# Four more columns summed on TensorE, stores issued by ScalarE, softmax steps set between product and sums

## The chip, the cores and the metric

One core of a Trainium2 chip runs the whole program. The metric is the device time of one execution in microseconds (us). Before the change the median of 6 runs is 426.52 us (425.56 to 428.74).

The engines named here: TensorE (PE, multiplies matrices; PEld is its loading of weights), VectorE (DVE), ScalarE (ACT), GpSimd (POOL) and SyncE (SP). The last three also issue DMA transfers, each on a queue of its own.

## The reference

`x` is 8 x 4160 x 192 and `weight_gen` 8 x 4160 x 8 x 7. The first part is a causal convolution whose weights differ at each position and for each of 8 heads of 24 channels; the second a maxout layer.

```
w   = softmax(weight_gen over its 7 taps)
y[b, s, h, :] = sum over k of w[b, s, h, k] * x[b, s - 6 + k, h, :]      # zeros ahead of s = 0
g   = maximum(y @ w1, y @ w2)              # w1, w2: 192 x 1024, 33280 rows
out = g @ w_out                            # w_out: 1024 x 192
```

## The kernel before, in words

**Layout.** The 33280 positions are split over 128 partitions, so each partition holds 260 consecutive positions, called columns. Columns are worked on in batches of 16 (17 batches, the last of 4). `pieces(b)` cuts a batch into parts, and `UNITS` lists them: batch 0 in four units of 4 columns, batch 1 in 4, 4 and 8, the others in 8 and 8, the last one of 4. A unit is what one product, one set of sums and one transposition handle.

**Softmax.** For a batch, `exp_sum` takes the exponentials on ScalarE (L126), `red` sums them over the taps on VectorE (L131), `ln` takes the logarithm on ScalarE (L134), `shift` subtracts it on VectorE (L139), and `weights` takes the exponential again on ScalarE (L147), now the finished weight in bf16, each value twice.

**Convolution.** `mul` multiplies seven shifted views of `x` by the weights into `m_t` (VectorE, L158). `adds` sums the seven taps in three instructions: taps 0 to 2 with 3 to 5 (L174), then L179, then L181, which writes `y_t`. The tile `m_t` has room for one batch and is taken anew from its pool (`pm`, one buffer) for every batch; L158 of a new batch therefore depends on the readers of the tile before it.

**Transposition.** TensorE needs the channels on the partitions. Most units are transposed by a DMA that SP issues (`transpose`, L190, from `y_t` to `yt`). The first six units, columns 0 to 23, take another way, `sum_transpose`: TensorE multiplies `m_t` by an identity matrix and sums the taps in PSUM as it goes (L220), and ScalarE copies the result (L225). For units 0 to 3 it sums all seven taps, for units 4 and 5 four, after VectorE's first sum only.

**Maxout.** max(y w1, y w2) w_out is computed as y (w1 w_out) + relu(y (w2 - w1)) w_out. A "tile" is an eighth of the hidden layer for a unit of 8 columns (for a unit of 4, two eighths for half of the columns); there are 260 tiles. `hid_tile` computes one on TensorE into PSUM (L252), `relu` brings it to SBUF on ScalarE (L262). When all tiles of a unit are there, `out_first` and `out_second` compute its columns of the result on TensorE (L304 with y, L292 with the relu), and `evac` copies them from PSUM to `o_t` on ScalarE (L348). `o_t` has room for 24 columns and is used in a ring.

**Order.** Every engine's order is written out by hand (`manual_schedule`); engines run in that order and wait for one another by semaphores. `GROUPS` cuts the tiles into groups of 2, from tile 12 on of 3. `OUTS` says which columns of the result are computed beside each group: none at first, then 2 or 4. `hidden(g, ...)` issues one group: all tiles but the last, `out_first`, their relus, the last tile, its relu, `out_second`, `evac`. `extra(t)`, called beside the group of tile t, issues what is due for later batches: products, sums and softmax steps on VectorE, exponentials on ScalarE, and the transposition of the next unit. `early` holds the same for the first groups.

**Loads and stores.** POOL issues the loads of `x` (L114, converted to bf16), the copy of the six columns that two batches share (L120), the loads of `weight_gen` (L104) and most stores (L362). In `transpose`, from unit 6 on, POOL first copies one element of the transposed unit (L198, `gate`), so it waits there until that transposition has landed, and issues the transfers behind it. `evac` collects finished columns in the list `stores`; those of the first groups and of the end are issued by ScalarE right away, all others by POOL behind the next gate.

Of the kernel before, what the change touches and what calls it, by code (L numbers as in the profile page):

```python
# [10 lines left out]
BF16 = mybir.dt.bfloat16  # L11
# [12 lines left out]
def kernel(  # L24
# [28 lines left out]
    def pieces(b):  # L53
        n = BATCHES[b][1]
        at, done = [], 0
        for w in {0: (4, 4, 4, 4), 1: (4, 4, 8)}.get(b, (8, 8) if n == 16 else (n,)):
            at.append((done, w))
            done += w
        return at
# [10 lines left out]
    GROUPS = [(t, 2) for t in range(0, 12, 2)]  # L70
    GROUPS += [(t, min(3, NT - t)) for t in range(12, NT, 3)]

# [25 lines left out]
    stores, transposed = [], [-1]  # L98
    wg_ts, xb_ts, e_ts, s_ts, en_ts, m_ts, y_ts, yt_ts = {}, {}, {}, {}, {}, {}, {}, {}
# [53 lines left out]
    def mul(b, o):  # L153

        n = dict(pieces(b))[o]
        if b not in m_ts:
            m_ts[b] = pm.tile([P, K * 16 * D], BF16, name="m_t", tag="m")
        nc.vector.tensor_tensor(  # L158
            out=m_ts[b][:, K * o * D:K * (o + n) * D],
# [5 lines left out]
    def adds(b, o, first=False):  # L165
# [3 lines left out]
        m_t = m_ts[b]  # L169
# [16 lines left out]
    def transpose(u):  # L186
# [8 lines left out]
        transposed.append(u)  # L195

        if u > 5:
            nc.gpsimd.tensor_copy(out=gate, in_=yt[:, 0:1])  # L198
            c = b + 1 if o == 0 else b + 2
            if o == 8 and c < NB:  # L200
                load_x(c, 0, min(8, BATCHES[c][1]))
            if o == 0 and c < NB and BATCHES[c][1] > 8:
                load_x(c, 8, BATCHES[c][1] - 8)
            if o == 0 and b + 3 < NB:
                load_wg(b + 3, nc.gpsimd)
            store(nc.gpsimd)
# [4 lines left out]
    def sum_transpose(u, taps=range(K)):  # L211
# [4 lines left out]
        for k in range(nb):  # L216
            for t in taps:
                for j in range(2):
                    at = (K * o + t * n + k // 3 + j * n // 2) * D + k % 3 * 64
                    nc.tensor.matmul(  # L220
                        yps[half(j), k * P:(k + 1) * P], lhsT=m_ts[b][:, at:at + 64],
# [108 lines left out]
    def evac(p, n):  # L330
# [15 lines left out]
        for qs in runs:  # L346
            c, h = place(qs[0])
            nc.scalar.copy(out=_sub(o, c % 24 * D, [[D, len(qs)], [h * D, 2], [1, D]]),  # L348
                           in_=_sub(tile_, at + (qs[0] - p) * D, [[D, len(qs)], [512, 2], [1, D]]))
        for q in range(p, p + n):  # L350
# [5 lines left out]
        if p < 12 or transposed[-1] == NU - 1:  # L356
            store(nc.scalar)

    def store(eng):

        for c, w in stores:
            eng.dma_start(  # L362
# [3 lines left out]
        stores.clear()  # L366
# [3 lines left out]
    OUTS, c = [], 0  # L370
    for t0, n in GROUPS:
        most = {2: 0, 3: 4}.get(len(OUTS), 2 if len(OUTS) < 10 or len(OUTS[-1]) == 4 else 4)
        OUTS.append([])
        while len(OUTS[-1]) < most and c < NT:
            u = column(c)[0]
            if TILES.index((u, 0)) + UNITS[u][2] > t0:
                break
# [338 lines left out]
```

## Time and profile before

| | before |
|---|---|
| median of 6 runs | 426.52 us |
| lowest, highest | 425.56, 428.74 us |
| profiled execution: its time | 434.07 us |
| its span in the profile | 432.0 us |
| TensorE busy | 405.0 us, 7261 matmuls |
| VectorE busy | 382.0 us, 176 instructions |
| ScalarE busy | 357.1 us, 411 instructions |
| POOL busy | 78.1 us, 130 instructions |
| moved by DMA | 66.07 MB, 153 GB/s on the mean |
| stores issued by POOL | 27, of 768 KB, median 8.8 us to landing |
| stores of 768 KB issued by ScalarE | 2, median 3.3 us to landing |
| transposes issued by SP | 30, median 6.4 us to landing |

The profile is of one execution; its time is the span and about 2 us around it. It is 7.5 us longer than the median, so a sum over its rows has to be set against 434.07 us first. A row of a timeline reads: start in us, duration in us, engine, line, operation, what it writes and reads, how many instructions are merged; in brackets the idle time of the engine ahead of it and what ended that.

### The profile page before, as it was taken

How to read it: one execution, taken by the hardware profiler on the slowest of the kernel's cores; microseconds unless marked ns; L12 is line 12 of the kernel's file. 1: busy time of each engine (PE TensorE's matmuls, PEld its weight loads, DVE VectorE, ACT ScalarE, POOL GpSimd, SP SyncE). 2: the span in 40 equal slices, each digit the busy share in tenths (PEclk: the TensorE clock that was granted, in tenths of full speed). 3: DMA queues.
4: the chain of work that ended last, by engine and by line, in shares of the span. 5: the costliest groups of instructions: out<-in, count | busy, mean ns of one | idle time of the engine just before them, and what ended most of it. 6: DMA issues, size and time to landing. Idle time of an engine off the chain costs nothing.

```text
span 432.0 us, 15756 instructions
## 1 busy us (share of the span) xinstructions
PE 405.0 (94%) x7261; PEld 324.1 (75%) x7261; DVE 382.0 (88%) x176; ACT 357.1 (83%) x411; POOL 78.1 (18%) x130
## 2 busy tenths in 40 slices
PE   7999999999989999899899999789679999999985
PEld 7789897787768777676677677567557777777785
DVE  5999999999999999999999999999939999997000
ACT  5897899998988889797788989678568989878771
POOL 1510011121401123122031223111020311220100
PEclk9999999999999999999999999999969999999999
DMA  8973376568499587888769776878985688574412
GB/s 249 262 168 125 76 174 149 118 105 162 80 238 168 126 222 135 149 124 189 160 119 233 172 135 142 156 157 102 224 168 125 132 163 174 58 211 122 156 74 111
DMA packets 61682, 66.07 MB, mean 153 GB/s; under 512 B 49169, under 2 KB 50065, under 8 KB 61616
## 3 DMA queue, kind: packets, MB, share of 16 engines
q0 software_dynamic: 12016, 45.34, 42.6%
q1 hardware_dynamic: 48016, 15.50, 24.2%
q10 hardware_dynamic: 1584, 4.23, 2.6%
q8 instruction: 56, 0.92, 0.9%
q14 instruction: 10, 0.08, 0.1%
HBM read 35.96 MB, written 25.56 MB: 142 GB/s over the span
## 4 chain that ended last, share of the span: by engine, by line
DVE 55%; PE 26%; DMA 12%; issue 3%; ACT 3%; ACTq 0%; POOL 0%; DVEq 0%; SPq 0%; POOLq 0%
DVE m_t L158 28%; PE op_ps L292 12%; DVE m_t L174 12%; PE hd L252 10%; DVE m_t L179 8%; DMA yt<-y_t 7%; DMA out_dram<-o_t 3%; DVE y_t L181 3%; DVE wg_t L139 3%; PE op_ps L304 2%; DVE sum_t L131 2%; DMA xb_t<-in_x_dram 1%; PE yps L220 1%; ACT rd_t L262 1%; DMA wg_t<-in_weight_gen_dram 1%
## 5 line engine op out<-in xcount | busy, mean ns | idle before, releaser
L262 ACT ACTIVATE rd_t<-hd 128x1024 bf16<-128x1024 f32 (+1 forms) x210 | 239.3, 1185 | 41.2 <-PE hd L252 39.7
L292 PE MATMUL op_ps<-wo,rd_t 64*128 64x192 bf16 x4160 | 211.3, 243 | 0.1
L252 PE MATMUL hd<-yt,wd 64*128 64x512 bf16 (+1 forms) x1584 | 191.1, 364 | 9.7 <-DMA yt<-y_t 7.3
L158 DVE TENSOR_TENSOR m_t<-xb_t,en_t 128x10752 bf16<-128x10752 bf16 (+1 forms) x36 | 187.3, 5206 | 7.6 <-ACT en_t L147 7.5
L292 PEld LDWEIGHTS <-rd_t 64*128 64x128 bf16 x4160 | 181.5, 94 | 16.6 <-issue 0.5
L252 PEld LDWEIGHTS <-wd 64*128 64x128 bf16 x1728 | 91.2, 94 | 53.7 <-issue 9.7
L198 POOL CAST gate<-yt 128x1 f32<-128x1 bf16 x30 | 27.7, 924 | 298.4 <-DMA yt<-y_t 298.4
L174 DVE TENSOR_TENSOR m_t<-m_t 128x4608 bf16<-128x4608 bf16 (+1 forms) x32 | 78.3, 2445 | 1.1
L348 ACT COPY o_t<-op_ps 128x384 f32<-128x384 f32 (+1 forms) x97 | 57.0, 599 | 22.6 <-PE op_ps L292 13.2
L304 PE MATMUL op_ps<-w,yt 64*128 64x192 bf16 x780 | 55.7, 244 | 9.0 <-ACT o_t L348 9.0
L304 PEld LDWEIGHTS <-yt 64*128 64x128 bf16 x780 | 38.4, 94 | 26.6 <-issue 11.5
L179 DVE TENSOR_TENSOR m_t<-m_t 128x3072 bf16<-128x3072 bf16 (+1 forms) x30 | 51.9, 1731 | 1.0
L147 ACT ACTIVATE en_t<-wg_t 128x896 bf16<-128x896 f32 (+1 forms) x36 | 34.6, 972 | 0.0
L181 DVE TENSOR_TENSOR y_t<-m_t 128x1536 bf16<-128x1536 bf16 (+1 forms) x30 | 28.3, 945 | 1.0
L338 DVE COPY o_t<-op_ps 128x192 f32<-128x192 f32 x1 | 0.4, 357 | 31.3 <-ACT o_t L338 31.3
L131 DVE TENSOR_REDUCE sum_t<-e_t 128x128 f32<-128x896 f32 (+1 forms) x17 | 17.6, 1037 | 2.6 <-ACT e_t L126 2.6
L139 DVE TENSOR_TENSOR wg_t<-wg_t,sum_t 128x896 f32<-128x896 f32 (+1 forms) x17 | 17.7, 1044 | 1.2 <-ACT sum_t L134 1.2
L114 POOL DMA_DIRECT2D xb_t<-in_x_dram x32 | 17.2, 536 | 9.4 <-ACT rd_t L262 6.9
L126 ACT ACTIVATE e_t<-wg_t 128x896 f32<-128x896 f32 (+1 forms) x17 | 15.9, 935 | 2.5 <-DMA wg_t<-in_weight_gen_dram 2.5
L362 POOL DMA_DIRECT2D out_dram<-o_t x27 | 14.4, 538 | 2.8 <-ACT o_t L348 2.5
L220 PE MATMUL yps<-ident,m_t 128*64 128x128 bf16 x432 | 13.4, 220 | 0.9 <-DVE m_t L158 0.9
L220 PEld LDWEIGHTS <-m_t 128*64 128x64 bf16 x432 | 12.4, 110 | 1.9 <-DVE m_t L158 1.1
(46 smaller groups left out, 93.8 us busy)
## 6 DMA issues: line engine op xcount, KB each, us to landing
out_dram<-o_t POOLq DMA_DIRECT2D x27, 768.0 KB, 8.8
xb_t<-in_x_dram POOLq DMA_DIRECT2D x28, 384.0 KB, 5.1
wg_t<-in_weight_gen_dram POOLq DMA_DIRECT2D x14, 448.0 KB, 6.5
xb_t<-xb_t POOLq DMA_DIRECT2D x16, 288.0 KB, 5.6
out_dram<-o_t ACTq DMA_DIRECT2D x6, 384.0 KB, 2.3
out_dram<-o_t ACTq DMA_DIRECT2D x2, 768.0 KB, 3.3
wg_t<-in_weight_gen_dram SPq DMA_DIRECT2D x2, 448.0 KB, 5.0
xs<-in_x_dram SPq DMA_DIRECT2D x2, 384.0 KB, 6.5
```

What stands on the lines that cost most here:

```text
L139: nc.vector.tensor_tensor(out=w_t, in0=w_t, in1=_sub(s_ts.pop(b), 0, [[1, TH], [0, K]]), op=ALU.subtract)
L147: nc.scalar.activation(out=_sub(en_ts[b], o * WGC * 2, [[2 * N, K], [2, N], [1, 2]]), in_=_sub(wg_ts[b], o * WGC, [[1, K], [K, N], [0, 2]] ...
L158: nc.vector.tensor_tensor(out=m_ts[b][:, K * o * D:K * (o + n) * D], in0=_sub(xb_ts[b], o * D, [[D, K], [1, n * D]]), in1=_sub(en_ts[b], o ...
L174: nc.vector.tensor_tensor(out=taps(0, 1, 3), in0=taps(0, 1, 3), in1=taps(3, 1, 3), op=ALU.add)
L179: nc.vector.tensor_tensor(out=taps(0, 2, 2), in0=taps(0, 2, 2), in1=taps(1, 5, 2), op=ALU.add)
L181: nc.vector.tensor_tensor(out=_sub(y_ts[b], o * D, [[64, 2], [P, 3 * w // 2], [1, 64]]), in0=taps(0, 1, 1), in1=taps(2, 1, 1), op=ALU.add,)
L220: nc.tensor.matmul(yps[half(j), k * P:(k + 1) * P], lhsT=m_ts[b][:, at:at + 64], rhs=ident, start=(t == taps[0]), stop=(t == taps[-1]), sk ...
L252: nc.tensor.matmul(hid_out(t, f, j), lhsT=wd[half(j), s * F + f * P:s * F + (f + 1) * P], rhs=_sub(yt_ts[u][half(j), :], (s + j) % 3 * P, ...
L262: nc.scalar.activation(out=rd[:, k * 1024:(k + n) * 1024], in_=hd[:, at:at + n * 1024], func=AF.Relu)
L292: return nc.tensor.matmul(op_out(c), lhsT=rd[half(r), k * 1024 + at:k * 1024 + at + P], rhs=wo[half(r), f * D:(f + 1) * D], start=False, s ...
L304: nc.tensor.matmul(op_out(c + j), lhsT=yt_ts[u][half(j), (3 * i + (s + j) % 3) * P:(3 * i + (s + j) % 3 + 1) * P], rhs=w10[half(j), s * D: ...
L348: nc.scalar.copy(out=_sub(o, c % 24 * D, [[D, len(qs)], [h * D, 2], [1, D]]), in_=_sub(tile_, at + (qs[0] - p) * D, [[D, len(qs)], [512, 2 ...
```

## The change

Six edits, made together:

- Batch 1 is cut into four units of 4 columns, like batch 0. Columns 24 to 31 are then units 6 and 7 and go through `sum_transpose` with four taps, as units 4 and 5 do. There are 37 units in place of 36.
- Groups of 2 tiles reach to tile 16, and `OUTS` is planned anew: the columns that are ready at each group are worked out from the end backwards.
- `m_t` is one tile for the whole kernel, not one per batch.
- `red` and `shift` stand between `mul` and `adds` in VectorE's order, not ahead of `mul`.
- On ScalarE, `exp_sum` and `weights` are issued five tiles earlier and `ln` six. The second part of a batch (`mul`, `adds`) is issued at tile 8 of a batch, not at tile 4, and a transposition one tile earlier; VectorE's and SP's own orders stay as they are but for the steps named.
- All stores but the very last are issued by ScalarE as soon as their columns are copied; POOL issues none. POOL's gate is there for every transposed unit, and one load of `x` for batch 3 moves ahead of the first gate.

```diff
-        for w in {0: (4, 4, 4, 4), 1: (4, 4, 8)}.get(b, (8, 8) if n == 16 else (n,)):
+        for w in (4, 4, 4, 4) if b < 2 else (8, 8) if n == 16 else (n,):
...
-    GROUPS = [(t, 2) for t in range(0, 12, 2)]
-    GROUPS += [(t, min(3, NT - t)) for t in range(12, NT, 3)]
+    GROUPS = [(t, 2) for t in range(0, 16, 2)]
+    GROUPS += [(t, min(3, NT - t)) for t in range(16, NT, 3)]
...
+    m_t = pm.tile([P, K * 16 * D], BF16, name="m_t")
...
-        if b not in m_ts:
-            m_ts[b] = pm.tile([P, K * 16 * D], BF16, name="m_t", tag="m")
...
-        if u > 5:
-            nc.gpsimd.tensor_copy(out=gate, in_=yt[:, 0:1])
...
-            store(nc.gpsimd)
+        nc.gpsimd.tensor_copy(out=gate, in_=yt[:, 0:1])
...
-        if p < 12 or transposed[-1] == NU - 1:
-            store(nc.scalar)
-
-    def store(eng):
-
         for c, w in stores:
-            eng.dma_start(
+            nc.scalar.dma_start(
...
-    OUTS, c = [], 0
-    for t0, n in GROUPS:
-        most = {2: 0, 3: 4}.get(len(OUTS), 2 if len(OUTS) < 10 or len(OUTS[-1]) == 4 else 4)
...
+    for g in range(len(GROUPS) - 2, 3, -1):
+        ready[g] = min(ready[g], ready[g + 1] - 2)
+    OUTS, c = [[], [], []], 0
+    for g in range(3, len(GROUPS)):
+        most = 4 if g == 3 else 2 if GROUPS[g][1] == 2 or len(OUTS[-1]) == 4 else 4
+        n = min(most, ready[g] - c)
...
     def rest_of_1():
+        mul(1, 8)
         shift(2)
-        mul(1, 8)
-        adds(1, 8)
+        adds(1, 8, True)
+        mul(1, 12)
+        red(3)
+        adds(1, 12, True)
...
-        3: (none, rest_of_1),
-        4: (lambda: (exp_sum(3), sum_transpose(4, (0, 1, 2, K - 1))), lambda: weights(2, 0)),
-        5: (lambda: sum_transpose(5, (0, 1, 2, K - 1)), lambda: transpose(6)),
-        6: (lambda: weights(2, 8), none),
+        3: (none, lambda: (exp_sum(3), rest_of_1())),
+        4: (lambda: sum_transpose(4, (0, 1, 2, K - 1)), lambda: weights(2, 0)),
+        5: (lambda: sum_transpose(5, (0, 1, 2, K - 1)), none),
+        6: (lambda: (weights(2, 8), ln(3), sum_transpose(6, (0, 1, 2, K - 1))), lambda: load_x(3, 0, 8)),
+        7: (lambda: sum_transpose(7, (0, 1, 2, K - 1)), none),
...
-            if c + 1 < NB:
-                red(c + 1)
             mul(c, 0)
+            if c + 1 < NB:
+                shift(c + 1)
             adds(c, 0)
-        if s == 4 and b + 2 < NB:
-            ln(b + 2)
-            shift(b + 2)
+        if s == 8 and b + 2 < NB:
             mul(b + 1, 8)
+            if b + 3 < NB:
+                red(b + 3)
             adds(b + 1, 8)
-        if k == 2 and 6 < u + 1 < NU:
+        if k == n // 4 - 1 and 7 < u + 1 < NU:
             transpose(u + 1)
 
-        for o, at in ((0, 13), (8, 17)):
+        for o, at in ((0, 8), (8, 12)):
...
-        c = (t - 9) // 16 + 3
-        if (t - 9) % 16 == 0 and 3 < c < NB:
+        if s == 14 and 3 < b + 3 < NB:
+            ln(b + 3)
+        c = (t - 4) // 16 + 3
+        if (t - 4) % 16 == 0 and 3 < c < NB:
             exp_sum(c)
```

## The prediction

> **What bounds the kernel now.** I read the page's first and fourth parts, then the timeline of VectorE, then that of TensorE and ScalarE with the idle time before each instruction, then busy time by stretch.
>
> ```profile
> PE 405.0 (94%) x7261; PEld 324.1 (75%) x7261; DVE 382.0 (88%) x176; ACT 357.1 (83%) x411; POOL 78.1 (18%) x130
> DVE 55%; PE 26%; DMA 12%; issue 3%; ACT 3%; ACTq 0%; POOL 0%; DVEq 0%; SPq 0%; POOLq 0%
> ```
>
> Two engines are nearly full. The chain runs over VectorE to about 277 us and over TensorE from 316 us. VectorE's timeline shows one unit of 8 columns:
>
> ```profile
> 131.79 0.96 DVE L181 TENSOR_TENSOR y_t<-m_t 128x1536 bf16<-128x1536 bf16 x1
> 132.67 1.08 DVE L139 TENSOR_TENSOR wg_t<-wg_t,sum_t 128x896 f32<-128x896 f32 x1
> 133.67 5.75 DVE L158 TENSOR_TENSOR m_t<-xb_t,en_t 128x10752 bf16<-128x10752 bf16 x1
> 139.46 2.56 DVE L174 TENSOR_TENSOR m_t<-m_t 128x4608 bf16<-128x4608 bf16 x1
> 142.05 1.76 DVE L179 TENSOR_TENSOR m_t<-m_t 128x3072 bf16<-128x3072 bf16 x1
> 143.84 0.96 DVE L181 TENSOR_TENSOR y_t<-m_t 128x1536 bf16<-128x1536 bf16 x1
> 144.72 1.08 DVE L131 TENSOR_REDUCE sum_t<-e_t 128x128 f32<-128x896 f32 x1
> ```
>
> The same line comes again after 143.84-131.79 = 12.05 us, without a pause. Look at the joints. A sum that reads what the instruction ahead wrote starts 0.03 us after its end (133.67+5.75 = 139.42, next 139.46). A softmax step that reads nothing of it starts 0.08 us before its end (131.79+0.96 = 132.75, next 132.67), and so does the product after the step.
>
> ```profile
> 177.72 0.82 PE L252 MATMUL hd<-yt,wd 64*128 64x512 bf16 x6 [1.34 <-DMA yt<-y_t]
> ...
> 289.20 0.82 PE L252 MATMUL hd<-yt,wd 64*128 64x512 bf16 x6 [1.18 <-DMA yt<-y_t]
> ...
> 315.24 0.80 ACT L348 COPY o_t<-op_ps 128x768 f32<-128x768 f32 x1 [6.85 <-DMA out_dram<-o_t]
> ...
> 316.09 0.67 PE L304 MATMUL op_ps<-w,yt 64*128 64x192 bf16 x6 [6.14 <-ACT o_t L348]
> ```
>
> From 128 to 289 us TensorE waits at one unit in two for the transposed sums, so VectorE sets the pace. I call "lag" the time from the end of L181 to TensorE's first L252 of that unit. Where it waits, the lag is 8.1 us (y ready 120.7, start 128.8), 8.8 (177.7), 8.7 (201.7) and 11.9 (289.2). At 315 us a late store held ScalarE for 6.85 us: TensorE idled 6.14 us and VectorE 7.29 (for weights queued behind that copy).
>
> ```profile
> 394.22 1.48 PE L252 MATMUL hd<-yt,wd 64*128 64x512 bf16 x12
> 402.86 1.47 PE L252 MATMUL hd<-yt,wd 64*128 64x512 bf16 x12
> ```
>
> These two lines lie six tiles apart: 8.64 us, or 11.52 per unit of eight. That is TensorE's own pace with work at hand, 0.5 us per unit better than VectorE's.
>
> The profiled execution took 434.07 us, 432.0 of it span (2.07 around). Unit 248 to 255, the last wide one, had its sums at 390.70+0.96 = 391.66 and began on TensorE at 400.89; from there to the end it is 31.1 us. Without the pause the sums would be ready at 391.66-7.29 = 384.4; with a lag of 9.0 the end is 384.4+9.0+31.1+2.07 = 426.6. That is the median of the runs (426.52), so I take the pause as peculiar to this execution (7.5 us above the median) and the bound as VectorE plus lag.
>
> **The change part by part.**
>
> *Columns 24 to 31 in two fours.* VectorE loses one chain of 8 (5.75+2.56+1.76+0.96, 11.0 us with joints) and gets two products and two first sums of 4: by the rows at 32.06 and 35.04, 2.95+1.36, less an overlap, 4.2 each, 8.4 in all. Gain on the path: 2.6 us. TensorE gets 2 x 48 matmuls of four taps:
>
> ```profile
> 37.89 1.53 PE L220 MATMUL yps<-ident,m_t 128*64 128x128 bf16 x48
> ```
>
> The next matmul starts at 39.35, so 1.46 each, +2.9 us. The hidden tiles of fours cost nothing more (24 of 256 wide in 1.49 us, 12 of 512 wide in 1.48, both two tiles). From 32 to 125 us TensorE pauses for little over 1 us in all, so these 2.9 us delay it in full; they are hidden only once it waits for VectorE. ScalarE gets two copies more (0.80 each, L225) in a stretch where it still waits 0.4 to 0.8 us per group for TensorE; SP has one transpose fewer.
>
> *Softmax steps between product and sums.* In the order after, each of 29 steps (L131 or L139) stands between L158 and L174. The sum no longer meets its producer's end, and the next product follows L181 directly. The product then must not wait for L181: with one m_t for the whole kernel it touches the other half, and no wait on VectorE is attached to it. The joints become -0.09 in place of +0.03: 0.12 x 29 = 3.5 us. [...] I take the rows, which show both joints in this kernel, and keep 0 as the other end.
>
> *Where the ScalarE and VectorE steps wait.* exp (L126) and weights (L147) come five tiles earlier in ScalarE's order, ln (L134) six. ScalarE is in order: relus (L262) stand behind them, and TensorE waits for relus. ln now needs a reduction that ends 6.8 us after the last L181; ScalarE gets there some 6.7 us after it in the tightest place (lag 9 less 2.3): about no wait, but a smaller lag would make one. exp needs weights that POOL asks for after the transposed unit lands: about 1.5 us plus 6.5 to landing, 8 after it; ScalarE is there 6.4 to 10.1 us after TensorE's start of that unit. So 0 to 2 us, once, as it only enlarges the lag. I put both into the lag: 9.0 rather than the 8.1 to 8.8 of the quiet stretches. Weights come earlier, so VectorE keeps some 5 us in hand even with TensorE 5 us further behind. If that is gone, VectorE waits on TensorE's pace.
>
> *Stores by ScalarE.* 27 issues leave POOL (0.54 us each, not on the path) and ScalarE gets them. Its own issues take 0.34 us:
>
> ```profile
> 60.70 0.35 ACTq L362 DMA_DIRECT2D out_dram<-o_t  x1
> ```
>
> and in 320 to 390 us:
>
> ```profile
> sum 70.00, PE 70.00 PEld 54.37 DVE 67.72 ACT 62.16 POOL 13.64; mean PE 10.00 PEld 7.77 DVE 9.67 ACT 8.88 POOL 1.95
> ```
>
> ScalarE idles 7.8 us in 70, 1.3 per unit, and 0.34 fits: cost 0. With no cover it is 0.34 per unit on TensorE's pace, 22 units from 128 us on, 7.5 us. POOL's stores wait for the next transposed unit and land 8.8 us after issue; ScalarE's two of that size take 3.3. So the 6.85 us pause should not recur, and a store no longer comes in pairs. [...] The rows: with both queues busy (60 to 72 us) the transpose landed in 6.4 us, in pairs of POOL stores in 8 to 9. [...] I take 0.
>
> *POOL and groups.* load_x(3) moves ahead of the first gate and needs only products done by 45 us; stores out of POOL's queue let loads go some 0.5 to 1 us earlier. Groups of two to tile 16 make 90 groups for 89; the results kept for the end are eight columns in both. 0 +- 0.5.
>
> *Sum.* Against the profiled 434.07: less the pause, 7.29 on VectorE, and 0.2 of lag (9.2 to 9.0), 426.6; less 2.6, less 3.5: 420.5. Two limits meet here. VectorE's: 384.4-6.1 = 378.3, lag 9, start of the last wide unit 387.3. TensorE's: it could have begun at 127.6 the unit it began at 128.8; +2.9+22 x 11.52 = 383.9. VectorE is later by 3.4 us, so it sets the end.
>
> **The rivals.**
>
> 1. *TensorE and ScalarE become the bound.* If the 0.34 us per unit shows in full, the start is 383.9+7.5 = 391.4 and the time 424.6; with half, about 421. For it: ScalarE is 89% busy. Against: TensorE does not pause in 320 to 390, even beside two softmax steps.
> 2. *The joints do not close.* Only 2.6 us remain: 424.0.
> 3. *Slower: transposes land late.* Stores, loads and transposes in three queues at once. The time before is reached when the lag is 15.1 us, and slower begins at 17.2 us; at 18, 429.5. For it: one transpose took 14.7 us already, and 11.9 at 289 us. Against: fewer stores at a time.
> 4. *Better:* landing in 6 us lets TensorE's limit decide: 417.2.
>
> **How the numbers follow.** Main 0.64 (420.5; 417.2 to 422.5, rival 4 within it), rival 2 0.10, rival 1 0.15, rival 3 0.11. What a measurement here can tell from no change is 0.5%, 2.1 us. Faster by more: 0.64+0.06+0.08 = 0.78; within: 0.04+0.06+0.02 = 0.12; slower: 0.01+0.09 = 0.10. The range 417.2 to 425.0 leaves out most of rival 3 and a little of rival 1.
>
> **What would show it.** Right: L158 starts repeat every 11.92 us; softmax rows start 0.09 before the end of L158; L220 counts 528; no wait of L348 for out_dram; the last wide unit's L181 ends near 378.3; TensorE waits for yt only in the second half. Wrong: gaps of VectorE ahead of L158 or L139, waits of L126 for wg_t, L134 for sum_t, or landings of yt above 12 us.

## The result, and the profile after

The changed kernel takes 423.87 us (median of 33 runs, 421.69 to 427.02) where the kernel before, on the same chips, takes 426.64 us. The ratio is 0.9932, 95% interval 0.9917 to 0.9948: faster by 2.8 us. The forecast was 420.5 us, a gain of 6.1. Direction and range held; less than half of the gain came. The profiled execution took 425.05 us (span 423.2).

Runs more than 1.5% above the fastest of the same kernel count in the medians below but not in the ratios, and since the profiles of a_steps2 and r_pe_late are of such runs, only landings, pauses and the time of tile 8 are taken from them.

First the page's first and fourth parts:

```profile
PE 407.4 (96%) x7405; PEld 329.9 (78%) x7405; DVE 377.1 (89%) x176; ACT 360.2 (85%) x416; POOL 70.4 (17%) x102
DVE 57%; PE 28%; ACT 7%; issue 3%; DMA 3%; ACTq 1%; SPq 0%; DVEq 0%
```

DMA had 12% of the chain before and has 3% now. TensorE has 144 matmuls more. VectorE's timeline over one unit:

```profile
145.33 0.96 DVE L179 TENSOR_TENSOR y_t<-m_t 128x1536 bf16<-128x1536 bf16 x1
146.21 5.75 DVE L157 TENSOR_TENSOR m_t<-xb_t,en_t 128x10752 bf16<-128x10752 bf16 x1
151.88 1.08 DVE L140 TENSOR_TENSOR wg_t<-wg_t,sum_t 128x896 f32<-128x896 f32 x1
152.88 2.55 DVE L172 TENSOR_TENSOR m_t<-m_t 128x4608 bf16<-128x4608 bf16 x1
155.46 1.76 DVE L177 TENSOR_TENSOR m_t<-m_t 128x3072 bf16<-128x3072 bf16 x1
157.25 0.96 DVE L179 TENSOR_TENSOR y_t<-m_t 128x1536 bf16<-128x1536 bf16 x1
```

The joints did close: 145.33+0.96 = 146.29, and the product starts at 146.21; the step starts 0.08 us before the product ends, the sum 0.08 before the step ends. The period is 157.25-145.33 = 11.92 us, as forecast. Here VectorE did what was asked of it. TensorE's waits tell why that is not the time:

```profile
PE op_ps L299 <- ACT o_t L343: 4.5, 8, 0.9
...
PE op_ps L287 <- issue: 1.2, 2, 0.9
PE hd L247 <- ACT rd_t L257: 0.9, 3, 0.3
```

There is no line for yt any more (before: 7.3 us in 6 waits). From its first tile to its last, TensorE never waits for VectorE or for a transposition directly. It works at its own pace and started late; VectorE's gain stands in front of it as lag.

Why, then, does the chain still have 57% on VectorE? It is followed back from the end, over TensorE to 356.8 us, and there it crosses to VectorE at a single place. ScalarE's `ln` waits for the last reduction of a batch, and a relu, a copy and TensorE wait behind it (ScalarE's row, then TensorE's):

```profile
354.92 0.23 ACT L135 ACTIVATE sum_t<-sum_t 128x32 f32<-128x32 f32 x1 [0.74 <-DVE sum_t L132]
```
```profile
356.80 0.42 PE L299 MATMUL op_ps<-w,yt 64*128 64x192 bf16 x6 [0.51 <-ACT o_t L343]
```

From this crossing the chain goes back over VectorE to 104 us. But TensorE lost only 0.51 us here, so a faster VectorE could hardly have brought it more than that.

To see this unit by unit I read from the traces where L179 of a unit ends ("sums"), where TensorE loads the first weights for the unit, and the lag between. (The loading can stand ahead of a wait for yt: in the profile of before it starts at 176.12 us for a product at 177.72, so there this lag is 1.6 us shorter than the one of the prediction.) Tile 72 stands after the start-up, tile 248 is the last wide unit (us from the start of the span; the names of the variants are told below):

| kernel | tile 8 | tile 72 | us per unit, 72 to 248 | sums of 248 | lag | tile 248 | from there to the end |
|---|---|---|---|---|---|---|---|
| before | 35.5 | 128.7 | 12.37 (with a pause) | 391.7 | 9.2 | 400.8 | 31.2 |
| changed | 38.7 | 135.6 | 11.58 | 382.4 | 7.9 | 390.3 | 32.9 |
| a_stores | 39.0 | 130.7 | 11.80 | 385.4 | 4.8 | 390.2 | 31.4 |
| u_stores | 36.0 | 132.1 | 11.70 | 378.9 | 10.6 | 389.5 | 32.6 |
| u_fours | 36.0 | 131.6 | 11.75 | 381.3 | 8.9 | 390.2 | 32.3 |
| r_dve | 37.0 | 133.6 | 11.69 | 380.5 | 10.3 | 390.8 | 32.6 |
| u_delay | 38.4 | 133.8 | 11.58 | 380.6 | 7.9 | 388.5 | 33.1 |

The two rows behind the changed kernel's figures for tile 248 (the second merges the loads of tiles 247 and 248, and the latter's six begin at 390.3):

```profile
381.45 0.96 DVE L179 TENSOR_TENSOR y_t<-m_t 128x1536 bf16<-128x1536 bf16 x1
```
```profile
389.77 1.06 PEld L247 LDWEIGHTS <-wd 64*128 64x128 bf16 x12
```

In the changed kernel the lag sinks from 19.8 us at tile 32 to 13.1 at tile 72 and 6.3 at tile 224. The forecast had VectorE's side set the end (sums 378.3, lag 9.0) and TensorE able to start tile 248 at 383.9. Both figures are off: the sums came at 382.4, TensorE at 390.3.

### The profile page after: what moved, and what is told of

It is laid out like the page before. It is cut to its first block, busy times and chain, and to the rows that moved or that the text cites. A ratio compares the mean times of both kernels' runs of the same rounds, so it can differ in the third digit from the quotient of the medians.

```text
span 423.2 us, 15949 instructions
## 1 busy us (share of the span) xinstructions
PE 407.4 (96%) x7405; PEld 329.9 (78%) x7405; DVE 377.1 (89%) x176; ACT 360.2 (85%) x416; POOL 70.4 (17%) x102
## 4 chain that ended last, share of the span: by engine, by line
DVE 57%; PE 28%; ACT 7%; issue 3%; DMA 3%; ACTq 1%; SPq 0%; DVEq 0%
DVE m_t L157 28%; DVE m_t L172 12%; PE op_ps L287 11%; DVE m_t L177 9%; PE hd L247 8%; ACT rd_t L257 4%; PE yps L215 3%; PE hdp L247 3%; DVE y_t L179 3%; DVE wg_t L140 3%; DVE sum_t L132 2%; PE op_ps L299 2%; DMA ws0E<-in_moe_w_dram 1%; DMA ws1T<-in_moe_w_dram 1%; ACT o_t L343 1%
## 5 line engine op out<-in xcount | busy, mean ns | idle before, releaser
L257 ACT ACTIVATE rd_t<-hd 128x1024 bf16<-128x1024 f32 (+1 forms) x206 | 234.6, 1184 | 31.5 <-PE hd L247 31.1
L247 PE MATMUL hd<-yt,wd 64*128 64x512 bf16 (+1 forms) x1584 | 187.3, 360 | 0.9 <-ACT rd_t L257 0.9
L247 PEld LDWEIGHTS <-wd 64*128 64x128 bf16 x1776 | 93.6, 94 | 41.8 <-issue 1.8
L194 POOL CAST gate<-yt 128x1 f32<-128x1 bf16 x29 | 34.7, 1197 | 284.3 <-DMA yt<-y_t 284.3
L343 ACT COPY o_t<-op_ps 128x384 f32<-128x384 f32 (+1 forms) x99 | 57.1, 587 | 11.9 <-PE op_ps L287 11.8
L299 PE MATMUL op_ps<-w,yt 64*128 64x192 bf16 x780 | 55.4, 243 | 4.5 <-ACT o_t L343 4.5
L299 PEld LDWEIGHTS <-yt 64*128 64x128 bf16 x780 | 38.6, 94 | 21.5 <-issue 6.7
L177 DVE TENSOR_TENSOR m_t<-m_t 128x3072 bf16<-128x3072 bf16 (+1 forms) x29 | 50.2, 1730 | 1.0
L333 DVE COPY o_t<-op_ps 128x192 f32<-128x192 f32 x1 | 0.4, 358 | 31.4 <-ACT o_t L333 31.4
L179 DVE TENSOR_TENSOR y_t<-m_t 128x1536 bf16<-128x1536 bf16 (+1 forms) x29 | 27.4, 944 | 1.0
L215 PE MATMUL yps<-ident,m_t 128*64 128x128 bf16 x528 | 17.4, 226 | 0.2 <-DVE m_t L157 0.2
L215 PEld LDWEIGHTS <-m_t 128*64 128x64 bf16 x528 | 16.1, 114 | 1.8 <-issue 1.5
L257 ACT ACTIVATE rd_t<-hdp 128x1024 bf16<-128x1024 f32 x16 | 15.7, 1025 | 1.6 <-PE hdp L247 1.5
```

The source lines that it names most:

```text
L177: nc.vector.tensor_tensor(out=taps(0, 2, 2), in0=taps(0, 2, 2), in1=taps(1, 5, 2), op=ALU.add)
L179: nc.vector.tensor_tensor(out=_sub(y_ts[b], o * D, [[64, 2], [P, 3 * w // 2], [1, 64]]), in0=taps(0, 1, 1), in1=taps(2, 1, 1), op=ALU.add,)
L215: nc.tensor.matmul(yps[half(j), k * P:(k + 1) * P], lhsT=m_t[:, at:at + 64], rhs=ident, start=(t == taps[0]), stop=(t == taps[-1]), skip_g ...
L247: nc.tensor.matmul(hid_out(t, f, j), lhsT=wd[half(j), s * F + f * P:s * F + (f + 1) * P], rhs=_sub(yt_ts[u][half(j), :], (s + j) % 3 * P, ...
L257: nc.scalar.activation(out=rd[:, k * 1024:(k + n) * 1024], in_=hd[:, at:at + n * 1024], func=AF.Relu)
L299: nc.tensor.matmul(op_out(c + j), lhsT=yt_ts[u][half(j), (3 * i + (s + j) % 3) * P:(3 * i + (s + j) % 3 + 1) * P], rhs=w10[half(j), s * D: ...
```

## The experiments

Ratios are to the kernel before on the same chip, with their 95% intervals. Differences of less than about 0.4% between variants are not resolved by them.

| variant | median us | ratio (interval) |
|---|---|---|
| changed kernel | 423.87 | 0.9932 (0.9917 to 0.9948) |
| u_steps: changed, steps ahead of the product | 430.91 | 1.0096 (1.0058 to 1.0134) |
| u_fours: changed, no fours for columns 24 to 31 | 424.33 | 0.9945 (0.9923 to 0.9967) |
| u_stores: changed, stores by POOL | 423.93 | 0.9910 (0.9882 to 0.9938) |
| a_stores: before, stores by ScalarE | 424.78 | 0.9924 (0.9893 to 0.9956) |
| a_steps: before, steps after the product, ln left in place | 433.43 | 1.0119 (1.0068 to 1.0170) |
| a_steps2: the same, ln mended | 422.86 | 0.9901 (0.9870 to 0.9931) |
| c_best: a_steps and a_stores | 426.97 | 0.9989 (0.9959 to 1.0019) |
| c_best2: a_steps2 and a_stores | 424.01 | 0.9941 (0.9921 to 0.9961) |
| a_fours: before, with the fours | 430.06 | 1.0092 (1.0052 to 1.0132) |
| a_fs: a_fours and a_stores | 430.91 | 1.0103 (1.0058 to 1.0148) |
| r_dve: changed, VectorE relieved | 423.98 | 0.9922 (0.9893 to 0.9952) |
| r_pe: changed, TensorE relieved early | 422.27 | 0.9896 (0.9859 to 0.9932) |
| r_pe_late: changed, TensorE relieved in the middle | 423.05 | 0.9901 (0.9870 to 0.9932) |
| r_act: changed, ScalarE relieved | 424.22 | 0.9933 (0.9904 to 0.9961) |
| u_delay: changed, stores one group later | 422.76 | 0.9922 (0.9888 to 0.9956) |
| c_delay: c_best2, stores one group later | 423.07 | 0.9913 (0.9874 to 0.9952) |
| r_late_delay: u_delay and r_pe_late | 422.29 | 0.9893 (0.9852 to 0.9933) |
| u_fours_delay: u_fours and u_delay | 424.03 | 0.9935 (0.9909 to 0.9961) |

### One part undone

**u_steps.** The steps back ahead of the product:

```diff
-            mul(c, 0)
             if c + 1 < NB:
                 shift(c + 1)
+            mul(c, 0)
...
-            mul(b + 1, 8)
             if b + 3 < NB:
                 red(b + 3)
+            mul(b + 1, 8)
```

> The changed kernel with only the softmax steps put back ahead of the product on VectorE (ScalarE's and TensorE's orders untouched). In the trace of the changed kernel the last wide unit has its sums at 382.4 us and starts on TensorE 7.9 us later; the smallest lag of the whole run is 6.3 us. My theory, that TensorE is the bound nearly to the end and VectorE only just catches up: each of 29 joints costs 0.12 us again, the period is 12.05 us, the sums come 3.5 us later (385.9), the lag sinks to its floor of 6.5 to 7.5 us, and some 1.5 to 3 us of the 3.5 appear: 425.5 to 427. If VectorE set the end of the changed kernel alone, all 3.5 appear: 427.4. If TensorE alone set it with room to spare, nothing: 423.9. [...]

Measured 430.91 us, above every figure expected and twice the loss that 29 joints explain. The period is 12.05 us again, so the order does matter. The rest lies early, in VectorE's timeline:

```profile
50.08 1.09 DVE L140 TENSOR_TENSOR wg_t<-wg_t,sum_t 128x896 f32<-128x896 f32 x1 [2.68 <-ACT sum_t L135]
...
64.31 1.08 DVE L132 TENSOR_REDUCE sum_t<-e_t 128x128 f32<-128x896 f32 x1 [2.09 <-ACT e_t L127]
```

A step moved ahead of the product is due 5.7 us earlier, and ScalarE, behind TensorE's pace, is not ready with ln and exp. VectorE's sums stood 3.6 us later than in the changed kernel at tile 72 (126.0 against 122.4), and at 12.05 us per unit it makes nothing good. So this variant is two things, joints and early waits, and I could not tell them apart by it.

**u_fours.** Columns 24 to 31 as one unit of eight again, groups of two to tile 12, the steps of `early` to match:

```diff
-        for w in (4, 4, 4, 4) if b < 2 else (8, 8) if n == 16 else (n,):
+        for w in (4, 4, 4, 4) if b < 1 else (4, 4, 8) if b == 1 else (8, 8) if n == 16 else (n,):
```

> The changed kernel with columns 24 to 31 as one unit of eight again, summed by VectorE and transposed by a DMA. TensorE has 96 matmuls less (2.9 us), VectorE 2.6 us more. If TensorE alone is the bound (theory 1), the time falls by the 2.9 us: 421.0. If the two are in balance (theory 2: TensorE is held by its late start, VectorE by waits for ScalarE steps that follow TensorE), TensorE gains and VectorE loses about the same: 423 to 425, with lags near 7 us all along and TensorE waiting for yt again. If VectorE plus lag were the bound as in the kernel before: 426.5.

424.33 us: the time is as the second theory has it. TensorE's start of tile 72 is 3.9 us earlier than in the changed kernel's trace, and it is all gone at tile 248.

**u_stores.** Stores behind the gate again:

```diff
             load_wg(b + 3, nc.gpsimd)
+        store(nc.gpsimd)
...
-            nc.scalar.dma_start(
+        if p < 16 or transposed[-1] == NU - 1:
+            store(nc.scalar)
```

> The changed kernel with its stores issued by POOL behind the gates again, as before the change. If the 0.34 us of each issue on ScalarE is what slows TensorE's pace (22 units from tile 72 on, at most 7.5 us), the time falls, to 420 to 423, and TensorE's period goes from 11.58 us to 11.4 or less. If ScalarE had room for them and the gain lay in the landings (transposes land after 4.3 us in the changed kernel, 6.4 before), landings go back to 6 to 8 us, the floor of the lag goes to 8 or 9 us, and the time rises to 425 to 427. Without any effect: 423.9.

423.93 us (ratio 0.9910 against 0.9932): not told apart from the changed kernel, but it gets there by another road. The transposes' landing, from the answers on their line, is 3.7/6.5/10.4 us (shortest/median/longest) against

```profile
DMA to landing us min/median/max: 3.3/4.3/7.2
```

in the changed kernel (the same line of its answer); the sums are 3.5 us earlier and the lag 10.6. From tile 72 to 176 TensorE's period is 11.56 us with ScalarE's stores and 11.56 without; the latter holds one wait of 0.6 us for a transposed unit. So at most some 0.05 us per unit of an issue's 0.34 shows in the pace.

### One part alone, and two

**a_stores.** Every store behind its copy, none behind the gate:

```diff
-        if p < 12 or transposed[-1] == NU - 1:
-            store(nc.scalar)
+        store(nc.scalar)
...
-            store(nc.gpsimd)
```

> The kernel before with one part of the change alone: every store issued by ScalarE right behind the copy that fills it, none by POOL. The kernel before is bound by VectorE plus the lag (8 to 9 us, landings of 6.4 us). If the stores of POOL are what makes the landings long, they fall to some 4.3 us, the lag to 6 to 7, and the time to 424.0 to 425.0. If the landings do not depend on the stores, or ScalarE is slowed as much: 426.6. If the issues on ScalarE show in full (0.34 us a unit on the pace of TensorE), TensorE's 11.52 becomes 11.86, still below VectorE's 12.05: no change either, so a rise above 427.5 would mean a wait that I do not see.

424.78 us, ratio 0.9924: alone it brings about what the whole change brings. Its DMA issues, and the first line of TensorE's waits:

```profile
out_dram<-o_t ACTq DMA_DIRECT2D x29, 768.0 KB, 4.6
...
yt<-y_t SPq DMA_TRANSPOSE x30, 4.3
```
```profile
PE hd L251 <- DMA yt<-y_t: 4.5, 5, 1.4
```

Landings fell from 6.4 to 4.3 us and the lag to 4 to 5 us over the last third. VectorE is still the bound here, now with a shorter road behind it.

**a_steps, c_best.** The steps behind the product, one `m_t`, ScalarE's steps where they were (c_best: stores by ScalarE too):

```diff
+        if s == 4 and b + 2 < NB:
+            ln(b + 2)
...
-            if c + 1 < NB:
-                red(c + 1)
             mul(c, 0)
+            if c + 1 < NB:
+                shift(c + 1)
             adds(c, 0)
```

> The kernel before with one part of the change alone: the softmax steps between product and sums, one m_t for the kernel; columns 24 to 31 stay one unit of eight, stores stay with POOL, ScalarE's steps and the grouping of the results stay where they were. VectorE's period should be 11.92 us instead of 12.05. By the rows of the joints the sums come 3.5 us earlier; TensorE, whose matmuls alone are 11.5 us per unit, can follow for about 3 us: 423.1 to 424.5. If only the parts together bring anything, or the landings behind POOL's stores (6.4 us) set the lag anew: 425 to 426.6.

> The kernel before with two parts of the change, steps between product and sums and stores by ScalarE, but without the two fours and with the grouping of the results and ScalarE's places as before. TensorE has 2.9 us less to do than in the changed kernel, and the end behind tile 248 took 31.4 us in the variant with ScalarE's stores alone against 33.0 in the changed kernel. If TensorE's work from its start on is the bound (theory 1), 419.5 to 421. If what was seen with the fours undone holds here too (both sides in balance, theory 2): 423 to 424.5.

433.43 and 426.97 us: both wrong. In each, VectorE waits 4.0 us at its first `shift` inside a product (until 59.6 and 59.8 us), for an ln that ScalarE has behind the relus of tile 20; a_steps has another such wait, of 5.0 us, at 232.8 us. Two more edits mend it: the first ln right behind the relus of tile 17 (the expectation has 14 by mistake), the others two tiles earlier.

```diff
-        if s == 4 and b + 2 < NB:
+        if s == 2 and b > 1 and b + 2 < NB:
             ln(b + 2)
...
+        7: (lambda: ln(3), none),
```

> The kernel before with the steps between product and sums alone (stores on POOL, no fours), the first ln mended in the same way. By the rows of the joints and without that wait the sums come 3.5 us earlier than in the kernel before: 423.1 to 424.5. If the landings behind POOL's stores (7.8 us each) and the pauses that late stores bring to ScalarE stay what they were with the steps alone (8.1 us of waits for out_dram in that trace): 426 to 430.

> The variant with steps between product and sums and stores by ScalarE, no fours, grouping as before, with one thing mended: in its trace VectorE waited 4.0 us for the first ln (L135) that came due inside a product, at the start, and its sums were 5.4 us later at tile 32 than in the variant with the stores alone (66.1 against 60.7 us), which it never made good. Here the first ln goes to ScalarE right after the relus of tile 14, the others at the third tile of a batch in place of the fifth. If that wait is what cost it, the sums of tile 248 come near 382.4 us and the time is 420.5 to 422.5. If not, 427.0 again.

422.86 us (0.9901, interval 0.9870 to 0.9931) with stores still on POOL: with that ln in time, the joints alone are worth some 4 us, which fits the forecast's 3.5 and is as much as the whole change brings. c_best2 misses: 424.01, where 420.5 to 422.5 was expected, though VectorE waits nowhere and its sums of tile 248 are ready at 381.6, 3.8 us earlier than in a_stores. TensorE waits more, not less:

```profile
PE hd L249 <- DMA yt<-y_t: 7.2, 7, 1.6
```

Its transposes land after 5.4 us (longest 8.9) where a_stores has 4.3 (7.3). Being earlier, more of them are issued together with a store: 11 of 28 within 1 us of a store's issue, in a_stores 4 of 28. This is taken up below.

**a_fours, a_fs.** The fours with their grouping; a_fs with stores by ScalarE too.

> The kernel before with one part of the change alone: columns 24 to 31 in two fours on TensorE, with the grouping of the results that belongs to it and one m_t; stores stay with POOL, the softmax steps stay ahead of the products, ScalarE's steps where they were. VectorE has 2.6 us less, TensorE 2.9 more. If parts do not add because each alone reaches the same limit (about 423 to 424), it alone gives 424.0, as the forecast's 2.6 us say. If its gain is lost at once in TensorE's start: 426 to 427.

> The kernel before with two parts: the two fours and stores by ScalarE; softmax steps ahead of the products and ScalarE's steps where they were. It differs from the variant of the changed kernel with the steps ahead of the product (430.9 us) by the places of exp, ln and weights in ScalarE's order. If those places made that one slow (its VectorE waited 6.1 us for ln and exp), it comes to 422.5 to 424.5. If steps ahead of the product do not go with the fours at all: 428 to 431.

430.06 us, above every figure expected, and 430.91. VectorE's timelines, a_fours and then a_fs:

```profile
63.69 1.09 DVE L140 TENSOR_TENSOR wg_t<-wg_t,sum_t 128x896 f32<-128x896 f32 x1 [4.73 <-ACT sum_t L135]
```
```profile
65.35 1.09 DVE L140 TENSOR_TENSOR wg_t<-wg_t,sum_t 128x896 f32<-128x896 f32 x1 [7.31 <-ACT sum_t L135]
```

The fours put VectorE ahead and TensorE, with ScalarE behind it, back; at the first ln they meet, and VectorE gives away more than the 2.6 us it won. The fours need the earlier ln that came with them in the change. With the places of ScalarE's steps held fixed, they lose.

### One engine relieved

These leave work out, as each expectation says. VectorE and TensorE early:

```diff
-        adds(1, 8, True)
...
-        adds(1, 12, True)
```
```diff
-        4: (lambda: sum_transpose(4, (0, 1, 2, K - 1)), lambda: weights(2, 0)),
+        4: (lambda: sum_transpose(4, (0,)), lambda: weights(2, 0)),
```

(the second for units 5 to 7 too).

> The changed kernel with VectorE relieved early: the first sums of columns 24 to 31 (two of 1.36 us, about 2.7 us) are left out, so VectorE is that much ahead from 55 us on; TensorE and ScalarE keep all their work. If TensorE is the bound, 423.9 within 1 us. If VectorE plus lag is, 421.2.

> The changed kernel with TensorE relieved early: the sums of the four units of four columns in columns 16 to 31 are taken over one tap, not four, which leaves out 4 x 36 matmuls, 4.4 us of TensorE by 1.46 us for 48, all before 60 us of the span. VectorE and ScalarE keep all their work. If TensorE is the bound from its start on (theory 1), tile 72 starts 4.4 us earlier, and the time falls by 2.5 to 4.4 us, up to where the lag meets its floor of 4.5 to 6 us: 419.5 to 421.4. If VectorE plus lag still sets the end (theory 2), the time stays at 423.9.

VectorE relieved: 423.98 us, nothing, although the sums of tile 248 came 1.9 us earlier. VectorE with its transpositions is not the bound of the changed kernel. TensorE relieved by 4.4 us: 422.27, 1.6 less by the medians (the intervals overlap). From tile 8 to 16, where all of the 4.4 us lie, TensorE took 16.36 us against 17.99 in r_dve: 1.6 came through, the rest turned into waits for ScalarE's copies of the sums (`PE op_ps L299 <- ACT yt L220`: 2.0 us). Behind TensorE's matmuls stands ScalarE's ring.

TensorE in the middle, then ScalarE:

```diff
-            for s in range(3):
+            for s in range(1 if 80 <= c < 128 else 3):
```
```diff
-                weights(c, o)
+                if c < 5:
+                    weights(c, o)
+                else:
+                    en_ts[c] = en_ts[c - 2]
```

> The changed kernel with TensorE relieved in the middle: for the results of columns 80 to 127 two of three slices of the product by w10 (L299) are left out, 4 of 6 matmuls for each of 24 pairs, 96 matmuls of 0.041 us, 3.9 us in all, all between about 145 and 225 us of the span. If TensorE is the bound there, tile 176 starts some 3.9 us earlier against tile 72; the end then moves by 1.5 to 3.9 us, less where the lag meets its floor: 420 to 422.4. If ScalarE is the bound there, 423.9.

> The changed kernel with ScalarE relieved: the exponentials of the weights (L148, 1.03 us each, about one per unit of eight) are left out from column 80 on, and the products read older weights. VectorE and TensorE keep all their work. If ScalarE's fullness is a part of the bound (TensorE waits 4.5 us for copies of results in the changed kernel, and its period is 11.58 us where its matmuls fill 11.5), the time falls by 1 to 4 us: 420 to 423. If TensorE's own stream is the whole bound: 423.9 within 0.7.

423.05 and 424.22 us, 0.8 less and 0.4 more than the changed kernel by the medians, neither resolved. r_act is the more telling. TensorE's period from tile 72 to 176 falls from 11.56 to 11.44 us, 1.6 us in 13 units, so ScalarE does hold it a little. Then in one unit all of that is given back: a transposition lands 2.0 us too late, and ScalarE stops at ln for VectorE's reduction:

```profile
283.84 0.31 ACT L135 ACTIVATE sum_t<-sum_t 128x128 f32<-128x128 f32 x1 [2.83 <-DVE sum_t L132]
```

The changed kernel passes the same place with little to spare. Its VectorE, then its ScalarE:

```profile
282.99 1.08 DVE L132 TENSOR_REDUCE sum_t<-e_t 128x128 f32<-128x896 f32 x1
```
```profile
284.74 0.30 ACT L135 ACTIVATE sum_t<-sum_t 128x128 f32<-128x128 f32 x1
```

282.99+1.08 = 284.07, and ln starts 0.67 us later. Whoever makes TensorE and ScalarE quicker by more than that meets this wait; at 354.92 us the changed kernel meets it itself.

### Stores moved off the transposes

In the 15 profiles of kernels whose stores are issued by ScalarE I set the time to landing of each transposition issued between 55 and 385 us against when the nearest store is issued:

| store issued, from the transposition's issue | transposes | median us to landing | longest |
|---|---|---|---|
| 2 to 1 us before | 59 | 4.9 | 8.6 |
| 1 to 0 us before | 44 | 5.8 | 8.7 |
| 0 to 1 us after | 49 | 6.3 | 9.3 |
| 1 to 2 us after | 50 | 4.4 | 12.2 |
| 2 to 3 us after | 41 | 4.0 | 7.7 |
| 3 to 4 us after | 30 | 3.7 | 5.8 |

The place of a store hangs on TensorE's progress, that of a transposition on VectorE's. So the lag sets which row applies, and in the changed kernel, as its lag sinks, the transposes come into the middle rows: 3.6 to 5.1 us to landing up to tile 144, 5.2 to 7.2 for seven of the eight units from tile 176 to 232. To test it as a cause, ScalarE issues each store one group later, some 4.3 us (the lines of u_delay; c_delay moves its own call in the same way):

```diff
-        stores = []
+        issue()
         for q in range(p, p + n):
...
+        if column(2 * (p + n - 1))[0] >= NU - 2:
+            issue()
```

> The variant with steps between product and sums and stores by ScalarE (no fours, first ln mended, 424.0 us), with one change: ScalarE issues each store one group later, behind the next copy of results, about 4.3 us after the copy that fills it. In the traces so far a transposed unit landed 4.0 us after issue where no store or load was under way (38 of 388), 6.3 with a store beside it for over 4 us, 8.7 with a store and loads. In that variant the transposes are issued at the same time as the stores, and TensorE waits 7.2 us for them. Theory 3, that this meeting is what gives the gain back: landings fall to some 4 to 4.5 us, TensorE's waits for yt to 2 us or less, the time to 419.5 to 421.5. If the landings do not depend on the stores' place (they are long because the queues are busy in all): 423.5 to 424.5.

> The changed kernel with each store issued by ScalarE one group later, about 4.3 us. Its transposes land 5 to 7 us after issue from tile 176 on, with 0.8 to 2 us in hand when TensorE comes, but TensorE waits for none. If TensorE's late start is the whole bound (theory 1), nothing changes: 423.9, with landings of about 4 us. If most runs lose a little at late landings (theory 3), 421.5 to 423.

u_delay: for the eight units of tiles 176 to 232 the landings fell from 4.4 to 7.2 us to 3.6 to 4.6 (and one of 7.9), and in the other seven the time from landing to TensorE's start grew from 0.8 to 2.0 us to 2.6 to 3.8. For the one of 7.9, beside a store again, TensorE waited 1.7 us. So in these units the meeting with a store is the cause of the long landings. The time is 422.76, 1.1 less by the medians and not resolved: the landings had been near to binding, not binding. (TensorE's period from tile 72 to 176 is 11.45 us in this trace, not 11.56, so a store's place in ScalarE's order may count for something too.) c_delay, 423.07, misses the 419.5 to 421.5 of its theory: TensorE ran 11 units at 11.54 us with the lag down to 4.1, nearly 6 us ahead of the changed kernel at tile 160. Then one transposition met a store all the same, landed after 8.2 us, and took everything back:

```profile
273.38 2.75 PE L249 MATMUL hd<-yt,wd 64*128 64x512 bf16 x12 [4.16 <-DMA yt<-y_t]
```
```profile
269.00:273.40 4.40, 0.24 (x8) 0.05 (x3) 4.40 (x3) 1.27 (x2) 0.03 (x1) 0.93 0.45 163
273.40:276.20 2.80, 2.80 (x16) 1.30 (x18) 2.73 (x3) 0.03 (x1) 1.73 (x3) 0.50 0.38 34
276.20:283.00 6.80, 6.80 (x130) 5.54 (x128) 6.80 (x3) 6.23 (x7) 1.64 (x2) 1.00 0.67 147
```

The second view is busy time by stretch (from:to, length, PE, PEld, DVE, ACT, POOL, then PEclk, the DMA share and GB/s). From 272.8 to 276.2 us TensorE had half its clock: 12 matmuls in 2.75 us in place of 1.48. The two units took 29.3 us, not 23.1.

> The changed kernel with each store one group later and with TensorE relieved by 3.9 us in the middle (for the results of columns 80 to 127 two of three slices of the product by w10 are left out). The same relief without the later stores brought 0.9 us (423.05), and its transposes landed 6.5 to 12 us after issue where TensorE had caught up. With the later stores alone the transposes have 3 to 4 us in hand. If TensorE's stream is one limit and the landings beside the stores the other, close behind it, the relief now comes through up to what is in hand: 419.5 to 421. If something else holds the end (ScalarE, or the tail): 422 to 423.

> The changed kernel without the two fours (columns 24 to 31 one unit of eight again) and with each store one group later: all computation is done. Without the later stores, undoing the fours gave 424.3 us: TensorE had 2.9 us less, VectorE 2.6 more, and the transposes landed 5 to 8 us after issue towards the end. If the landings are what took that gain, TensorE now starts its last wide unit 2 to 3 us earlier than the 388.5 of the changed kernel with later stores, and the time is 420 to 421.5. If fours or not makes no difference because VectorE falls behind as much: 422.5 to 424.

422.29 and 424.03 us: no break-through. Up to tile 168 r_late_delay ran 2.3 us ahead of u_delay (135.4 against 137.7 us from tile 72), then lost 3.6 in two units: a landing of 7.1 us and an ln that waited 2.57. In u_fours_delay the landings are short (median 4.0) and TensorE waits for none, but ScalarE and TensorE show:

```profile
259.63 0.31 ACT L135 ACTIVATE sum_t<-sum_t 128x128 f32<-128x128 f32 x1 [2.57 <-DVE sum_t L132]
```
```profile
261.60 0.66 PE L299 MATMUL op_ps<-w,yt 64*128 64x192 bf16 x6 [2.34 <-ACT o_t L343]
```

ln stands ahead of a relu and a copy in ScalarE's order, TensorE waits for the copy, and half a clock (granted 0.50) follows from 261.5 to 264.9 us.

The interval of every variant that is faster by the median overlaps that of the changed kernel. What r_act, u_delay, c_delay, r_late_delay and u_fours_delay share in their traces is that a gain is kept until the lag is down to between 4 and 7 us, and is then lost in part or in full at one of two places: ln ahead of its reduction, or a transposition beside a store.

## Why the prediction was right and wrong

**The joints: right.** 0.12 us each, 11.92 us per unit, some 4 us of the time where they act alone. The prediction kept 0 as the other end of this edit; no run shows it. The step and the sum start 0.08 us ahead of the end of what stands before them (151.88 against 151.96, 152.88 against 152.96), and with the steps put back ahead of the product the period is 12.05 us again (u_steps).

**The fours on VectorE: right** in size (sums of tile 72 at 121.34 us without them in u_fours, 118.95 with them in u_stores: 2.4), but they do not stand alone: without the earlier ln the kernel loses some 4 us by them, and in the changed kernel's own trace waits ate the gain (122.4).

**Stores by ScalarE, cost 0: right** within 0.05 us a unit, and no copy waits for an earlier store any more. **Gain 0: wrong.** The stores, for which the prediction says "I take 0", are one of the two parts, with the joints, that each bring about the whole gain alone: landings 6.4 to 4.3 us in a_stores. Where a transposition and a store by ScalarE are issued together, a landing does take up to 2.6 us more (6.3 us on the median, against 3.7 with the store 3 to 4 us later), but with POOL's stores, behind the gate with the loads, it was worse over all units: 6.5 us on the median in u_stores, 4.3 in the changed kernel.

**"I put both into the lag": wrong.** Waits of VectorE for exp and ln are not lag; they delay the sums themselves. Three of them, 0.30, 1.84 and 1.62 us:

```profile
66.72 1.08 DVE L132 TENSOR_REDUCE sum_t<-e_t 128x128 f32<-128x896 f32 x1 [1.84 <-ACT e_t L127]
...
104.19 1.09 DVE L140 TENSOR_TENSOR wg_t<-wg_t,sum_t 128x896 f32<-128x896 f32 x1 [1.62 <-ACT sum_t L135]
```

are 3.8 of the 4.1 us by which the sums of tile 248 missed 378.3; in u_stores, where VectorE waited for these only 0.3 us, they came at 378.9. The remark that "a smaller lag would make one", a wait of ln, named one of the two places at which later gains were lost, and gave it no price.

**TensorE's limit, 383.9, and "VectorE is later by 3.4 us, so it sets the end": the step that failed.** TensorE began tile 248 at 390.3, 6.4 us later, without having waited for a transposed unit. The three terms of that sum were each too small.

(1) The start, 3.2 us. Tile 8 began that much later than in the profile of before. About 1.6 of it is half clock (2.18 us at 23.52 and 3.46 at 25.63 for the matmuls that took 1.50 and 2.54 before), and most of the rest two pauses of 0.49 and 0.87 us for which the profile shows no wait ("issue"); the profile of before has neither in this stretch:

```profile
24.20:27.60 3.40, 3.40 (x54) 2.92 (x50) 3.40 (x3) 3.40 (x6) 0.00 (x0) 0.50 0.54 177
```
```profile
22.19 0.22 PE L542 MATMUL tp<-ident,w1E 128*128 128x128 bf16 x1 [0.49 <-issue]
...
35.95 0.51 PE L287 MATMUL op_ps<-wo,rd_t 64*128 64x192 bf16 x8 [0.87 <-issue]
```

(The first view is a stretch, read as under "Stores moved off the transposes".) Such pauses come in kernels of either grouping, 2.16 and 0.96 us in a_stores, 2.05 in r_pe, none in u_stores. Over all 20 profiles tile 8 begins between 35.5 and 39.0, and the profile of before has the earliest. So this term is not shown to be the change's own; the forecast was built on the most favourable start, and this execution took 1.2 us more than the median.

(2) Tile 8 to 72, 1.9 us: 96.8, against 93.2-1.2+2.9 = 94.9 in the forecast's sum. Half of it is pauses, 2.0 us in place of the 1.0 in the profile of before; I had added nothing for them because "TensorE pauses for little over 1 us in all". The other half is TensorE's own work: without pauses this stretch took 94.9 us against 91.0, so the fours cost it nearer 3.9 us than 2.9.

(3) The pace, 1.3 us: 11.58 us per unit, not 11.52, over 22 units. 3.2+1.9+1.3 = 6.4.

A fourth lies behind both limits: the end took 32.9 us, not 31.1. TensorE's part is 0.7 us longer, 0.4 of it in two waits for a copy (0.95 and 0.82 us, before 0.46 and 0.89), and what follows its last matmul 1.0. The old grouping had ends of 31.2 to 33.0 us in its profiles, so the grouping alone does not explain it. I took TensorE's best stretch for its pace, and its start from an execution in which nothing had pushed it.

**The rivals.** Rival 1 named the right engines, TensorE and ScalarE, but its price, the 0.34 us of a store shown in full, is not what happened; that its 424.6 is nearest in time is luck. Rivals 2 and 3 did not occur. (The 11.9 us at 289 that rival 3 names is a lag; that transposition landed after 11.7.) Rival 4 had the mechanism: landings fell below 6 us and TensorE's limit decided. Its 417.2 rests on the same 383.9 and fell with it.

What stays open: how much of the last 3 us is TensorE's stream and how much its ring with ScalarE. Relieving either gave at most 1.6 us, inside the intervals. It stays open, too, what makes the pauses and the half clock at the start, and why single transposes still landed after 7 to 8 us with the stores moved: they fell in with a later store, but the runs do not show how far loads had a part.

## What to carry to other kernels

When a bound engine is relieved, work out the limit of the next one from its start, its pace and its end over the whole run, not from its best stretch: here the second engine's limit lay 6.4 us later than such a stretch made it, and 2.8 us of a forecast 6.1 came. If several single edits each give about the same gain and do not add, look for a second limit close behind the first; that it is one and the same for all has to be read from each trace (a_stores was still bound by VectorE, the changed kernel was not). A step that is moved within one engine's order shifts the moment at which another engine must have delivered (the first waits were 2.68 us in u_steps, 4.0 in a_steps); look for the first instance, where the start-up leaves the least room, and for every place where one engine passes another with less than 1 us to spare.

## What the runs showed of the hardware

**Half clock after a pause.** In these traces the clock record has two values, 1.0 and 0.5, and half clock comes in pieces of 3.41 us (24.2 to 27.6 us in the changed kernel) or twice that (6.83, from 312.9 to 319.7 us before), the piece at the very end of a trace apart. Of 14 pauses of TensorE of 2 us or more past the first 15 us in the 20 profiles, the five of 2.66 us and above (2.66, 2.91, 2.98, 4.16, 6.14) were each followed by half clock for 3.4 us or 6.8; of the nine between 2.0 and 2.6, two. Two more pieces, at 24.2 us in the changed kernel and at 23.6 in c_delay, follow no pause over 0.5 us since 12 us, so half clock came without a longer pause as well. By the same record TensorE's pause of 6.14 us in the profile of before cost more than its length, as 3.6 us of work at half clock followed, and in c_delay a wait of 4.16 us cost 6.2 in its two units. In the changed kernel the 6 of 33 executions with a granted clock of 0.992 or 0.993 take 425.8 us on the mean, the others 423.5.

**Stores by queue.** A store of 768 KB landed 8.2 us after POOL's issue in u_stores and 4.6 us after ScalarE's in the changed kernel. The two differ in their moment as well, as POOL's stand beside its loads.
